# Sparse attention and a rational MLP on one core: new blocks for local and strided heads, transposes and loads moved between engines, and the last two chunks exchanged

## The chip, the cores and the metric

One of the eight cores of a Trainium2 chip runs the whole program. The metric is the device time of one execution in microseconds (us). Three executions of the kernel before took 433.36, 435.61 and 437.36 us; the median, 435.61 us, is the time before.

## The reference

Eight batches, eight heads, 576 positions, head size 64. Heads 0 to 3 are local (a query sees itself and the 31 keys ahead of it), heads 4 to 7 are strided (a query sees the earlier keys with the same position modulo 32). The result of attention, 4608 rows of 512, goes through two matrix products with a rational function between them:

```python
mask_local = (rel >= 0) & (rel < 32)
mask_strided = (rel >= 0) & (pos[None, :] % 32 == pos[:, None] % 32)
attn = softmax(where(mask, q @ k.T / 8, -1e9)); x = attn @ v     # (4608, 512)
h = x @ w_in                                                      # 512 -> 2048
g = (a0 + a1*h + a2*h**2 + a3*h**3) / (1 + |b0|*|h| + |b1|*h**2)
out = g @ w_out                                                   # 2048 -> 512
```

## The kernel before

Every instruction is recorded by `add(engine, ..., deps, cost, key)`. A list scheduler (`Program.schedule`) then fixes the order on each engine from those costs and keys; on the chip each engine works through its list in order and waits on semaphores. So a wait holds up all that stands behind it on the same engine. P = 36 is the step of the keys from one batch to the next.

**Attention of a batch.** `loads(b)` brings q, k and v from HBM on POOL's queue, with a cast to bf16: `qn`, `kn` (positions 0 to 511), `qm`, `km` (the last 64), `vt` and `v4` for local heads, `vs` and `w4` for strided ones; two buffers of each. `scores(b)` goes in rounds through a PSUM tile `psS` (batches 0 and 1 use `psA` and `psH` as well): TensorE transposes q and k with the identity `IDN` (`turn_s` for strided heads into `sT`, `turn_l` for local heads into `qL` and `kL`, `turn_m` for the last 64 positions), ScalarE or VectorE copies the result out. A score round then lays the mask into PSUM with two matmuls against `IDN`, adds the products of q and k, and ScalarE's Exp writes the probabilities. There are three strided rounds (`score_s`, into `ES`), two local ones (`score_l`, blocks of 128 queries by 128 keys, into `EL1`) and one for what crosses from block to block (`score_o`, into `EL2`, `EL3`). A position is split as p = 4*p' + g, with four residues g, so that a strided head needs only the keys of its own residue.

`attend(b)` makes five tiles T of 128 rows (T = 4 holds the last 64 positions): matmuls into `psA` (the 65th column of v is one and gives the sum), then VectorE's reciprocal (L747) and product (L749) into one of three buffers `XR`, then a DMA transpose on SP's queue (L764) into `XT`, which holds the features of one chunk in the partitions, two buffers. The tiles T = 4 of all batches are gathered in `XT8`. In a strided head a tile holds 32 rows of each residue, so `psA` gets them by 16 matmuls of 32 columns.

**The MLP.** Nine chunks of 512 rows; chunk 8 is `XT8`. `dense1(c)`: 16 groups of four matmuls through three PSUM banks `psH`, each copied to `HB` by ScalarE (L813); then VectorE makes the rational function in nine passes over up to eight groups (L821 to L852), with ScalarE's Ln and Exp (L833, L836) in place of the division. `dense2(c)`: four output tiles m of 16 matmuls into `psO`, copied to `OS` by ScalarE and stored by SP: four stores of 32 rows per tile (L867), for chunk 8 eight stores of 16 rows (L874). The last chunk uses four PSUM banks at once. `Win` and `Wout` come by one DMA each (L441, L445). TensorE starts with 14 matmuls on zeros, and in batch 0 one more stands behind each round.

Of the kernel before, what the change touches and what calls it, by code (L numbers as in the profile page):

```python
# [264 lines left out]
def bass_strided_sparse_attn__then__act_rational_pade_kernel(nc, q, k, v, moe_w_in, moe_w_out, moe_a, moe_b, out):  # L265
# [19 lines left out]
    EOFF = 5.0  # L285

# [6 lines left out]
    sT = A("sT", [128, 2, 2, 4, NP], BF)  # L293
    qL = A("qL", [128, 2, S], BF)
    kL = A("kL", [128, 2, S], BF)
    NV = 2
    vt = [A(f"vt{i}", [128, 4, 4, VS], BF) for i in range(NV)]
    v4 = [A(f"v4{i}", [64, 4, VS], BF) for i in range(NV)]
    w4 = [A(f"w4{i}", [128, 4, VS], BF) for i in range(NV)]
    vs = [A(f"vs{i}", [128, 4, 4, VS], BF) for i in range(NV)]  # L300
    NE = 2
    EL1 = [[A(f"EL1_{i}_{p}", [128, 2, 4, 128], BF) for p in range(2)] for i in range(NE)]
    EL2 = [A(f"EL2_{i}", [128, 2, 2, 4, 4, 32], BF) for i in range(NE)]
    EL3 = [A(f"EL3_{i}", [64, 2, 2, 4, 32], BF) for i in range(NE)]
    ESW = 8 * NP + 64
    ES = [A(f"ES_{i}", [128, 2, ESW], BF) for i in range(NE)]
# [4 lines left out]
    NXT = 2  # L311
    XT = [A(f"XT{i}", [128, NK1, CH], BF) for i in range(NXT)]
    XT8 = A("XT8", [128, NK1, B * 128], BF)
# [12 lines left out]
    ML1 = A("ML1", [128, 512], BF)  # L326
    ML2 = A("ML2", [128, 384], BF)
    MS1 = A("MS1", [128, 3 * NP], BF)
    MS2 = A("MS2", [128, 2 * NP + 64], BF)
# [11 lines left out]
    ar = np.arange(128)  # L341
    part = np.arange(128)
    d1 = (4 * (ar % 32) + ar // 32)[None, :] - part[:, None]
    m1 = np.where((d1 >= 0) & (d1 < STRIDE), 0.0, NEG)
    ml1 = np.tile(m1, (1, 4))
    ml2 = np.full((128, 2, 4, 4, 8), NEG)
    ml3 = np.full((128, 2, 4, 16), NEG)
    for g in range(4):
        for i in range(16):
            dd = 4 * i + g - part  # L350
            ok = (dd >= 0) & (dd < STRIDE) & (part < 64)
            ml3[ok, :, g, i] = 0.0
            dd = 128 + 4 * i + g - part
            ok = (dd >= 0) & (dd < STRIDE)
            if i < 8:
                ml2[ok, :, :, g, i] = 0.0
            else:
                assert not ok.any()
    ml2 = np.concatenate([ml3.reshape(128, -1), ml2.reshape(128, -1)], axis=1)
    dp = np.arange(NP)[None, :] - part[:, None]  # L360
    ms = np.where((dp >= 0) & (dp % 8 == 0), 0.0, NEG)
    ms1 = np.tile(ms, (1, 3))
    iq = np.arange(16)[None, :]
    ik = (part % 32)[:, None]
    mlo = np.where((ik < 16) & (iq >= ik) & ((iq - ik) % 8 == 0), 0.0, NEG)
    ms2 = np.concatenate([np.tile(ms, (1, 2)), np.tile(mlo, (1, 4))], axis=1)
# [17 lines left out]
    for dst, arr, nm, g_, ev in ((IDN, np.eye(128), "c_idn", gI, idn), (MS1, ms1, "c_ms1", gM, msk_ev),  # L384
                                 (MS2, ms2, "c_ms2", gM, msk_ev), (ML1, ml1, "c_ml1", gM, msk_ev),
                                 (ML2, ml2, "c_ml2", gM, msk_ev)):
# [29 lines left out]
    memset(ZB, OS[NO - 1][:, :], 0.0, key=-950.0)  # L416
    for i in range(NV):
        memset(vt[i], vt[i][:, :, :, 64:65], 1.0)
        memset(vs[i], vs[i][:, :, :, 64:65], 1.0)
        memset(v4[i], v4[i][:, :, 64:65], 1.0)  # L420
        memset(w4[i], w4[i][:, :, 64:65], 1.0)
    for i in range(NE):
        memset(EL2[i], EL2[i].rearrange("x a q t g c -> x (a q t g c)"), 0.0, cost=1.2)
        memset(EL3[i], EL3[i].rearrange("x a q g c -> x (a q g c)"), 1.0)

# [4 lines left out]
    ch_w1 = chan("c_w1")  # L430
    ch_w2 = chan("c_w2")
# [5 lines left out]
    g1 = ch_w1.group()  # L437
    g2 = ch_w2.group()

    def load_win():  # L440
        add("POOL", (lambda e: e.dma_start(Win[:, :, :], w_in.rearrange("(a p) f -> p a f", p=128))),  # L441
            [], 1.0, -960.0, g1, 12.0)

    def load_wout():
        add("POOL", (lambda e: e.dma_start(Wout[:, :, :], w_out.rearrange("(f p) o -> p f o", p=128))),  # L445
            [], 1.3, -900.0, g2, 12.0)

    def loads(b):
# [17 lines left out]
        if b == 0:  # L466
            for x, src, dst, dsm in srcs:
                big(x, src, dst, 4, 8, parts[x][0], key + x, 1.9)
            for x, src, dst, dsm in srcs:
                small(x, src, dsm, parts[x][1], key + 2 + x)  # L470
            for x, src, dst, dsm in srcs:
                big(x, src, dst, 0, 4, gg[x], key + 4 + x, 1.9)
            for x in range(2):
                n_ev[x, b] = {"s": parts[x][0].ops, "m": parts[x][1].ops, "l": gg[x].ops}
# [7 lines left out]
        base = [v_free[i], ini[id(vt[i])], ini[id(vs[i])], ini[id(v4[i])], ini[id(w4[i])]]  # L482
        key = (b - 1.9) * P if b > 1 else -990.0 + 50 * b
        for h in range(4):
            add("POOL", (lambda e, b=b, i=i, h=h: e.dma_start(  # L485
                vs[i][:, h, :, 0:64],
                v[b, 4 + h, 0:512, :].rearrange("(p g) d -> p g d", g=4))),
                base, 0.85, key, gv, 1.1)
        for g in range(4):
            add("POOL", (lambda e, b=b, i=i, g=g: e.dma_start(  # L490
                w4[i][32 * g:32 * g + 16, :, 0:64],
                v[b, 4:8, 512:576, :].rearrange("h (p g) d -> g p h d", g=4)[g])),
                base, 0.65, key, gv, 0.15)
        for h in range(4):
            add("POOL", (lambda e, b=b, i=i, h=h: e.dma_start(  # L495
                vt[i][:, :, h, 0:64],
                v[b, h, 0:512, :].rearrange("(t p) d -> p t d", p=128))),
                base, 0.85, key, gv, 1.1)
        add("POOL", (lambda e, b=b, i=i: e.dma_start(
            v4[i][:, :, 0:64],  # L500
            v[b, 0:4, 512:576, :].rearrange("h s d -> s h d"))),
            base, 0.7, key, gv, 0.5)
# [3 lines left out]
    s_free = [None]  # L506
    a_free = [None]
    h_free2 = [None]
    h_free = [None] * NHP
# [15 lines left out]
    q_free = [[]]  # L525
# [10 lines left out]

    def scores(b):
# [8 lines left out]
        ring = ["S", "A", "H"] if b == 0 else ["S", "A"] if b == 1 else ["S"]  # L546

# [6 lines left out]
        def turn_round(build, x, part, evacs):  # L554
# [6 lines left out]
            free[0] = [evac(eng, dst, src(ps), [o, q_free[0]], key, n) for eng, dst, src, n in evacs]  # L561
            return free[0]

        def score_round(msk, width, build, exps, deps):
# [5 lines left out]
            for (o, l, r) in build(ps):  # L570
# [4 lines left out]
            o2 = [add("ACT", (lambda c, dst=dst, src=src(ps): c.activation(dst, src, AF.Exp, scale=0.125)),  # L575
                      [o1, E_free[es]], 0.2 + n * 0.000833, key - EOFF) for dst, src, n in exps]
            free[0] = o2
            evs.extend(o2)


        dep = []
        depl = []

        def turn_s(x, eng):
            dep.append(turn_round(
                lambda ps: [mm(ps[:, gh, 128 * h:128 * h + 128], nat[x][:, 4 + h, 128 * gh:128 * gh + 128], IDN[:, :], True, True)
                            for gh in range(2) for h in range(4)],
                [x], "s", [(eng, sT[:, x, :, :, 0:128], lambda ps: ps.rearrange("x e (h p) -> x e h p", h=4), 1024)]))
# [13 lines left out]
        def turn_m():  # L602
            ev = turn_round(small, [0, 1], "m", [
                ("DVE", sT[:, :, :, :, 128:144].rearrange("x q e h p -> x q (e h) p"),
                 lambda ps: ps[:, :, 0:128].rearrange("x q (n p) -> x q n p", p=16), 256),
                ("DVE", qL[:, :, 512:576], lambda ps: ps[:, 0, 128:256].rearrange("x (a n) -> x a n", a=2), 128),
                ("DVE", kL[:, :, 512:576].rearrange("x a (p g) -> x a g p", g=4),
                 lambda ps: ps[:, 1, 128:256].rearrange("x (a g p) -> x a g p", a=2, g=4), 128)])
            dep.append(ev[0])
            depl.append([ev[1], ev[2]])  # L610

        def turn_l(x, eng):
            if x == 0:
                e = [(eng, qL[:, a, 0:512].rearrange("x (t g p) -> x g t p", t=4, g=4),
                      lambda ps, a=a: ps[:, a, :].rearrange("x (g t p) -> x g t p", g=4, t=4), 512) for a in range(2)]
            else:
                e = [(eng, kL[:, :, 0:512].rearrange("x a (p g) -> x a g p", g=4),
                      lambda ps: ps.rearrange("x a (g p) -> x a g p", g=4), 1024)]
            depl.append(turn_round(
                lambda ps: [mm(ps[64 * hh:64 * hh + 64, a, 128 * g:128 * g + 128],  # L620
                               nat[x][:, 2 * a + hh, 64 * g:64 * g + 64], IDN[:, :], True, True)
# [369 lines left out]
```

## Time and profile before

| what | value |
|---|---|
| median of three executions | 435.61 us |
| profiled execution, its own time | 437.65 us |
| its span, first to last instruction | 435.9 us |
| busy: TensorE, VectorE, ScalarE | 367.6, 329.0, 305.4 us |
| mean granted TensorE clock | 0.93 |
| first matmul of dense1, chunk 0 | 45.38 us |
| last copy of an output tile ends | 421.84 us |

Times inside an execution are counted from the start of the span. A busy share is taken over the whole span, and stages differ: at the start DMA works and the engines wait, in the middle three engines are almost full, at the end only stores are left. So the span is read stage by stage. In the views "x16" is a count of instructions, "a <- b" in front of a number names who was waited for, PEld is the load of weights, and SPq and POOLq are the queues that issue DMAs.

### The profile page before, as it was taken

What the parts mean: (1) busy time and instruction counts of PE and PEld (TensorE: products, weight loads), DVE (VectorE), ACT (ScalarE), POOL (GpSimd) and SP (SyncE); (2) the same over time, 40 slices, a digit from 0 to 9 for tenths busy, and PEclk for the clock granted to TensorE, in tenths of its full rate; (3) what the DMA queues carried; (4) which work ended last, traced back from release to release, by engine and by line L of the source; (5) the groups of instructions that cost most, each with busy time, mean ns of one, the idle gap of its engine ahead of it and who ended that gap; (6) DMA issues with size and microseconds to landing.
All of it is one profiled execution on the core that took longest, in us unless ns stands there. A gap on an engine that the chain in (4) does not pass through costs nothing.

```text
span 435.9 us, 7966 instructions
## 1 busy us (share of the span) xinstructions
PE 367.6 (84%) x3417; PEld 175.6 (40%) x3417; DVE 329.0 (75%) x309; ACT 305.4 (70%) x338; POOL 107.4 (25%) x144
## 2 busy tenths in 40 slices
PE   6751877679996999799989999999999997998760
PEld 2330332334552454355435444553454442343320
DVE  3421197960599589689996989796989999999920
ACT  2320398926794899789978897879897798849510
POOL 9985211008208402900580064000000000000000
PEclk9875698969999999999999999999999999899895
DMA  9999998029929923952594265221123101012012
GB/s 130 182 192 166 199 110 108 15 29 96 115 54 127 94 49 47 147 81 50 67 149 74 48 85 69 61 50 26 26 48 85 28 23 48 25 44 54 24 35 64
DMA packets 92260, 34.05 MB, mean 78 GB/s; under 512 B 66112, under 2 KB 87104, under 8 KB 92224
## 3 DMA queue, kind: packets, MB, share of 16 engines
q0 software_dynamic: 62144, 18.37, 42.0%
q1 hardware_dynamic: 30080, 15.16, 16.2%
q8 instruction: 27, 0.44, 0.5%
q14 instruction: 9, 0.07, 0.1%
HBM read 37.17 MB, written 9.44 MB: 107 GB/s over the span
## 4 chain that ended last, share of the span: by engine, by line
PE 49%; DVE 25%; DMA 11%; ACT 9%; issue 3%; SPq 1%; DVEq 0%
PE psH L518 20%; PE psO L518 14%; PE psS L518 10%; DMA XT<-XR 9%; PE psA L518 6%; DVE UU L827 4%; DVE T L852 3%; DVE T L843 3%; DVE T L847 3%; ACT kL L529 2%; DVE XR L749 2%; ACT UU L833 2%; DVE T L845 2%; DVE UU L824 2%; ACT UU L836 2%
## 5 line engine op out<-in xcount | busy, mean ns | idle before, releaser
L518 PE MATMUL psH<-XT,Win 128*128 128x512 bf16 x576 | 147.5, 393 | 18.9 <-DMA XT<-XR 16.8
L518 PE MATMUL psO<-Wout,T 128*128 128x512 bf16 x528 | 133.9, 384 | 8.7 <-ACT OS L917 4.9
L813 ACT ACTIVATE HB<-psH 128x512 bf16<-128x512 f32 x144 | 84.3, 600 | 58.8 <-PE psH L518 57.7
L518 PEld LDWEIGHTS psH<-XT,Win 128*128 128x128 bf16 x576 | 55.0, 100 | 87.0 <-issue 16.3
L833 ACT ACTIVATE UU<-UU,cst 128x2048 bf16<-128x2048 bf16 x36 | 71.5, 1998 | 7.1 <-DVE UU L827 7.0
L518 PEld LDWEIGHTS psO<-Wout,T 128*128 128x128 bf16 x528 | 47.1, 98 | 65.6 <-ACT OS L917 9.1
L836 ACT ACTIVATE UU<-UU 128x2048 bf16<-128x2048 bf16 x36 | 68.5, 1912 | 0.1
L821 DVE TENSOR_SCALAR T<-HB 128x4096 uint16<-128x4096 uint16 (+1 forms) x20 | 22.4, 1121 | 38.6 <-ACT HB L813 38.6
L852 DVE TENSOR_TENSOR T<-T,UU 128x4096 bf16<-128x4096 bf16 (+1 forms) x20 | 41.3, 2063 | 4.0 <-ACT UU L836 4.0
L485 POOL DMA_DIRECT2D vs<-in_v_dram x32 | 27.4, 861 | 63.9 <-PE psA L518 63.5
L847 DVE TENSOR_TENSOR T<-T,HB 128x4096 bf16<-128x4096 bf16 (+1 forms) x20 | 41.4, 2069 | 0.3
L827 DVE TENSOR_TENSOR UU<-UU,T 128x4096 bf16<-128x4096 bf16 (+1 forms) x20 | 41.4, 2069 | 0.3
L843 DVE TENSOR_TENSOR T<-T,HB 128x4096 bf16<-128x4096 bf16 (+1 forms) x20 | 41.3, 2067 | 0.2
L457 POOL DMA_DIRECT2D qn<-in_q_dram x9 | 8.7, 965 | 89.7 <-PE psS L518 88.9
L749 DVE TENSOR_TENSOR XR<-psA,RC 128x512 bf16<-128x512 f32 x40 | 27.4, 686 | 3.2 <-DMA XT<-XR 3.0
L917 ACT ACTIVATE OS<-psO 128x512 f32<-128x512 f32 x33 | 20.0, 606 | 12.7 <-PE psO L518 12.2
L495 POOL DMA_DIRECT2D vt<-in_v_dram x32 | 26.1, 847 | 0.0
L575 ACT ACTIVATE ES<-psS 128x864 bf16<-128x864 f32 (+1 forms) x20 | 17.0, 852 | 12.5 <-PE psS L518 11.0
L840 DVE TENSOR_SCALAR T<-HB,coef 128x4096 bf16<-128x4096 bf16 (+1 forms) x20 | 24.8, 1238 | 0.3
L824 DVE TENSOR_SCALAR UU<-T,coef 128x4096 bf16<-128x4096 bf16 (+1 forms) x20 | 24.6, 1230 | 0.3
L845 DVE TENSOR_SCALAR T<-T,coef 128x4096 bf16<-128x4096 bf16 (+1 forms) x20 | 23.6, 1182 | 0.3
L747 DVE RECIPROCAL RC<-psA 128x8 f32<-128x8 f32 x40 | 8.1, 203 | 20.8 <-PE psA L518 20.7
(111 smaller groups left out, 391.7 us busy)
## 6 DMA issues: line engine op xcount, KB each, us to landing
out_dram<-OS SPq DMA_DIRECT2D x128, 64.0 KB, 1.7
qn<-in_q_dram POOLq DMA_DIRECT2D x7, 512.0 KB, 6.8
kn<-in_k_dram POOLq DMA_DIRECT2D x7, 512.0 KB, 5.8
vs<-in_v_dram POOLq DMA_DIRECT2D x32, 64.0 KB, 6.3
vt<-in_v_dram POOLq DMA_DIRECT2D x32, 64.0 KB, 3.5
Win<-in_moe_w_in_dram POOLq DMA_DIRECT2D x1, 2048.0 KB, 13.4
Wout<-in_moe_w_out_dram POOLq DMA_DIRECT2D x1, 2048.0 KB, 26.2
out_dram<-OS SPq DMA_DIRECT2D x32, 32.0 KB, 1.7
```

Source lines behind the costliest of these rows:

```text
L485: add("POOL", (lambda e, b=b, i=i, h=h: e.dma_start(vs[i][:, h, :, 0:64], v[b, 4 + h, 0:512, :].rearrange("(p g) d -> p g d", g=4))), base ...
L518: return lambda e: e.matmul(out_ap, l, r, start=start, stop=stop, skip_group_check=True)
L749: o3 = add("DVE", (lambda d, rc=rc, x=x: d.tensor_tensor(x.rearrange("x (h d) -> x h d", h=8), psA[:, :, 0:64], rc[:, :, :].to_broadcast([ ...
L813: o2 = add("ACT", (lambda a, hb=hb, hi=hi, fi=fi: a.activation(hb[:, fi, :], psH[hi], AF.Copy)), [o1, hb_free[ig % NHB]], 0.6, key - HOFF)
L824: d2 = add("DVE", (lambda d, gn=gn, u=u, t3=t3: d.tensor_scalar(u[:, 0:gn, :], t3[:, 0:gn, :], b1_ap, b0_ap, op0=Alu.mult, op1=Alu.add)), ...
L827: d3 = add("DVE", (lambda d, gn=gn, u=u, t3=t3: d.tensor_tensor(u[:, 0:gn, :], u[:, 0:gn, :], t3[:, 0:gn, :], op=Alu.mult)), [d2], ctt, ke ...
L833: ln = add("ACT", (lambda a, u=u, sl=sl: a.activation(u[:, sl, :], u[:, sl, :], AF.Ln, bias=cst[:, 0:1], scale=1.0)), [d3, cons], 0.28 + H ...
L836: ex = add("ACT", (lambda a, u=u, sl=sl: a.activation(u[:, sl, :], u[:, sl, :], AF.Exp, scale=-1.0)), [ln], 0.28 + HG * CH * 0.000833, key ...
L843: d5 = add("DVE", (lambda d, gn=gn, hb=hb, t3=t3: d.tensor_tensor(t3[:, 0:gn, :], t3[:, 0:gn, :], hb[:, 0:gn, :], op=Alu.mult)), [d4], ctt ...
L845: d6 = add("DVE", (lambda d, gn=gn, t3=t3: d.tensor_scalar(t3[:, 0:gn, :], t3[:, 0:gn, :], a_ap[1], None, op0=Alu.add)), [d5], cts, key + ...
L847: d7 = add("DVE", (lambda d, gn=gn, hb=hb, t3=t3: d.tensor_tensor(t3[:, 0:gn, :], t3[:, 0:gn, :], hb[:, 0:gn, :], op=Alu.mult)), [d6], ctt ...
L852: d9 = add("DVE", (lambda d, gn=gn, t3=t3, u=u: d.tensor_tensor(t3[:, 0:gn, :], t3[:, 0:gn, :], u[:, 0:gn, :], op=Alu.mult)), [d8, lns], c ...
```

## The change

- **Local heads**: nine blocks of 64 queries by 96 keys (the 64 of the block and 32 ahead; `kL` gets zeros at both ends, `vt` becomes [96 keys, 9 blocks]). A block needs no second matmul for what crosses its edge, so `EL2`, `EL3`, `v4` and `score_o` go.
- **Strided heads**: a tile T < 4 now holds all 128 positions of residue T, so that four matmuls of 128 columns take the place of 16 of 32. Rows of local and strided heads stand in another order in `XT`; dense1 reads the two local parts of `XT` in runs of 16 elements. An output tile is then one residue, and one store of 128 rows takes the place of four.
- **Five mixed score rounds** in place of six: `score_0` (what is left of the last 64 strided positions, and six local blocks) into `E0`, and `score_1(h)` for h = 0 to 3 (strided head 4+h and three local blocks) into `E1`. Their order of work: `turn_l`, `turn_m`, `score_0`, then `score_1`.
- **Transposes**: from batch 2 on, `turn_s` becomes two DMA transposes of 128x1024 on SP's queue (`turn_sd`, L594). For batches 0 and 1 the transpose of `XR` goes from DMA to TensorE and ScalarE's copy. The tile T = 4 takes two smaller DMA transposes (`XT8l`, `XT8s`).
- **Buffers and parts**: three `XT` in place of two; `Win` in four DMAs, `Wout` in two, each with a semaphore of its own.
- **Order of chunks**: 0 to 6, then 8, then 7; in batch 7 tile T = 4 goes first.

```diff
+    TORD = {7: (4, 0, 1, 2, 3)}
+    XD = 2
+    XP = 2
...
-    NXT = 2
+    NXT = 3
...
+        def turn_sd(x):
+            g = ch_t[x].group()
+            o = add("SP", (lambda e: e.dma_start_transpose(
+                sT[:, x, :, :, 0:128].rearrange("x h g p -> x (h g) p"),
+                nat[x][:, 4:8, :].rearrange("x h c -> x (h c)"))),
+                [n_ev[x, b]["s"], st_old], 2.0, base - 20 + x, g, 1.2)
+            uses[x].append(o)
+            dep["s", x] = [o]
...
+        def local(ps, off, units):
+            return [(ps[:, hh, off + WIN * u:off + WIN * u + WIN],
+                     kL[64 * hh:64 * hh + 64, a, WIN * t:WIN * t + 128],
+                     qL[64 * hh:64 * hh + 64, a, WIN * t:WIN * t + WIN])
+                    for u, (t, a) in enumerate(units) for hh in range(2)]
...
+            if T < 4:
+                gh, j = divmod(T, 2)
+                for h in range(4):
+                    makers.append(mm(psA[:, 4 + h, 0:65], E1[es][:, h, j, gh * NP:gh * NP + 128],
+                                     vs[iv][:, h, T, 0:65], h == 0, True))
...
+            if b < XP:
+                bank, free = (psO, o_free) if (b or T % 2) else (psH[2], h_free3)
...
+                o4 = add("PE", makers, [o3, free[0]], 0.3, key - 1.0)
...
+    CORD = [0, 1, 2, 3, 4, 5, 6, 8, 7]
...
+                    elif kk < 2:
+                        r = XT[c % NXT][:, kk, :].rearrange("x (t g p) -> x g t p", g=4, p=16)
...
-            dst = out[576 * c + 128 * m:576 * c + 128 * m + 128, :].rearrange("(p g) o -> g p o", g=4)
-            for g in range(4):
-                add("SP", (lambda e, dst=dst, osl=osl, g=g: e.dma_start(
-                    dst[g], OS[osl][32 * g:32 * g + 32, :])), [ev], 0.75, key - 60, go, 0.2)
+            dst = out[576 * c:576 * c + 512, :].rearrange("(p g) o -> g p o", g=4)[m]
+            add("SP", (lambda e: e.dma_start(dst, OS[osl][:, :])), [ev], 0.75, key - 60, go, 0.9)
```

Two places show how the order moves. TensorE, from the fourth attention tile of batch 2 to the first dense1 matmuls of chunk 2, before (`vt0`, `vs0`: values of batch 2; `XT0` is chunk 2's, `XT1` chunk 1's, `T30` to `T32` hold chunk 0's function):

```order
L518 MATMUL psA<-vs0,ES_0 32x65 x16
L518 MATMUL psO<-Wout,T32 128x512 x4
L518 MATMUL psS<-IDN,qn1 64x128 x16
L518 MATMUL psA<-vt0,EL2_0 128x65 x4
L518 MATMUL psA<-v40,EL3_0 128x65 x4
L518 MATMUL psA<-vs0,ES_0 16x65 x16
L518 MATMUL psA<-w40,ES_0 16x65 x16
L518 MATMUL psO<-Wout,T30 128x512 x4
L518 MATMUL psS<-IDN,kn1 64x128 x16
L518 MATMUL psO<-Wout,T31 128x512 x4
L518 MATMUL psH<-XT0,Win 128x512 x4
```

Between the fourth tile and chunk 2 stand three groups of four dense matmuls, two turns and the fifth tile. The same place now (`XT2` is chunk 2's; the fourth tile and one group of chunk 1's dense1 stand just ahead of the first row):

```order
L511 MATMUL psO<-Wout,T32 128x512 x4
L511 MATMUL psS<-M1,IDN 128x480 x2
L511 MATMUL psS<-sT 128x144 x4
L511 MATMUL psS<-qL,kL 128x64 x6
L511 MATMUL psA<-vt0,E1_0 64x65 x4
L511 MATMUL psA<-vs0,E1_0 16x65 x16
L511 MATMUL psA<-w40,E0_0 16x65 x16
L511 MATMUL psS<-M1,IDN 128x480 x2
L511 MATMUL psS<-sT 128x144 x4
L511 MATMUL psS<-qL,kL 128x64 x6
L511 MATMUL psO<-Wout,T30 128x512 x4
L511 MATMUL psH<-XT2,Win 128x512 x4
```

Two whole score rounds of batch 3 have moved in between the fourth tile and chunk 2. On SP's queue, the transposes of batch 2's tiles and what stands among them, now (`sT<-qn0`, `sT<-kn0` are batch 4's):

```order
L768 DMA_TRANSPOSE XT2<-XR0 128x4x128
L768 DMA_TRANSPOSE XT2<-XR1 128x4x128
L875 DMA out_0_dram<-OS1 128x512
L594 DMA_TRANSPOSE sT<-qn0 128x8x128
L768 DMA_TRANSPOSE XT8l<-XR2 128x2x64
L768 DMA_TRANSPOSE XT8s<-XR2 128x2x128
L594 DMA_TRANSPOSE sT<-kn0 128x8x128
L875 DMA out_0_dram<-OS2 128x512
```

Before, this queue held only `XT` and `XT8` transposes and stores; now batch 4's transposes of q and k stand among them, and one of the stores and the fifth tile's transposes are behind a wait for batch 3's last score round.

More of the change, by code (lines that the diff above doesn't have):

```diff
@@ L338, in bass_strided_sparse_attn__then__act_rational_pade_kernel @@
     psO = Pa("psO", [128, 512], F32)
[L341 to L347, printed above, removed]
-    for g in range(4):
[L349 to L360, printed above, removed]
-    ms = np.where((dp >= 0) & (dp % 8 == 0), 0.0, NEG)
[L362 to L366, printed above, removed]
+    part = np.arange(128)[:, None]
+    wc = (4 * (np.arange(WIN) % 16) + np.arange(WIN) // 16)[None, :]
+    mw = np.where((wc - part + PADK >= 0) & (wc - part + PADK < STRIDE), 0.0, NEG)
+    dp = np.arange(NP)[None, :] - part
+    ms = np.where((dp >= 0) & (dp % 8 == 0), 0.0, NEG)
+    dp = np.arange(16)[None, :] - part
+    mlo = np.where((part < 16) & (dp >= 0) & (dp % 8 == 0), 0.0, NEG)
+    m0 = np.concatenate([np.tile(mlo, (1, 8)), np.tile(mw, (1, 6))], axis=1)
+    m1 = np.concatenate([np.tile(ms, (1, 2)), np.tile(mw, (1, 3))], axis=1)
     def const(name, arr):
@@ L612, in turn_l @@
+            dep["m"] = ev
         def turn_l(x, eng):
[L613 to L622 removed]
@@ L684, in scores @@
+        if by_dma:
+            turn_sd(0)
+            turn_sd(1)
+        turn_l(0, "ACT")
+        turn_l(1, "DVE" if b == 0 else "ACT")
         turn_m()
         if b == 0:
-            turn_l(0, "ACT")
-            turn_l(1, "DVE")
-        for r in range(3):
-            score_s(r)
+            score_0()
+        if not by_dma:
+            turn_s(0, "ACT")
+            turn_s(1, "DVE")
         if b:
-            turn_l(0, "ACT")
-            turn_l(1, "ACT")
-        for a in range(2):
-            score_l(a)
@@ L695, in scores @@
-        score_o()
+            score_0()
+        for h in range(4):
+            score_1(h)
         for x in range(2):
             n_free[x][i] = uses[x]
-        q_free[0] = list(evs)
+        st_free[0] = st_use
+        l_free[0] = l_use
         if b == 0:
@@ L791, in dense1 @@
         f0 = 0
-        for gn in sizes(c):
+        for gn in sizes(n):
             ig = ng[0]
```

366 lines of the change are left out of this document (182 added, 184 removed).

## The prediction

> **What bounds the kernel now.** I read the page first, then the busy time stage by stage, then who waited for whom, and last single stretches of the timeline.
>
> ```profile
> span 435.9 us, 7966 instructions
> PE   6751877679996999799989999999999997998760
> ...
> 45.00:100.00 55.00, 41.92 (x430) 19.60 (x433) 38.83 (x45) 36.49 (x39) 5.20 (x8) 0.82 0.74 91
> 100.00:320.00 220.00, 208.89 (x2203) 103.63 (x2202) 182.02 (x165) 185.49 (x212) 65.41 (x81) 0.99 0.61 75
> 320.00:416.00 96.00, 88.53 (x469) 38.48 (x467) 94.05 (x70) 73.39 (x75) 0.00 (x0) 0.96 0.16 41
> 416.00:435.90 19.90, 5.11 (x24) 2.14 (x22) 1.38 (x2) 1.19 (x2) 0.00 (x0) 0.76 0.22 53
> ```
>
> The columns of the last rows are the stretch, its length, then busy time of TensorE, its weight loads, VectorE, ScalarE and POOL, the granted clock, DMA. Four stages with four limits. Up to 45 us attention of batch 0 runs as one chain and nothing is full but DMA. From 100 to 320 us TensorE is the fullest, 208.9 of 220 us; VectorE (182.0) and ScalarE (185.5) each have over 34 us to spare. From 320 to 416 VectorE is full (94.05 of 96). After that only stores are left.
>
> **The start.**
>
> ```profile
> 14.14 0.83 POOL L441 DMA_DIRECT2D Win<-in_moe_w_in_dram  x1
> DMA to landing us min/median/max: 13.4/13.4/13.4
> 6.97 0.61 PE L518 MATMUL psS<-IDN,qn 128*128 128x128 bf16 x8
> 25.58 0.24 PE L518 MATMUL psA<-vt,EL_0_0 128*128 128x65 bf16 x2 [0.95 <-ACT EL_0 L575]
> 27.13 12.58 SPq L764 DMA_TRANSPOSE XT<-XR  x5
> 32.19 0.21 DVE L747 RECIPROCAL RC<-psA 128x8 f32<-128x8 f32 x1 [1.07 <-PE psA L518]
> 35.37 0.69 DVE L749 TENSOR_TENSOR XR<-psA,RC 128x512 bf16<-128x512 f32 x1 [2.98 <-DMA XT<-XR]
> 45.38 7.19 PE L518 MATMUL psH<-XT,Win 128*128 128x512 bf16 x20 [7.88 <-DMA XT<-XR]
> L813 ACT ACTIVATE HB<-psH 128x512 bf16<-128x512 f32 x144 | 84.3, 600 | 58.8 <-PE psH L518 57.7
> ```
>
> Attention's first tile starts at 25.58; the fourth has its sums at 32.40, but its product waits 3 us for a buffer that a DMA transpose still reads, and chunk 0 starts only at 45.38, behind DMA. `Win` is there at 14.1 + 13.4 = 27.5, so it isn't what chunk 0 waits for. With the change these transposes are on TensorE. The four tiles are spaced about 2.0 us now (the fourth's sums are 6.8 us behind the first tile's start); four transposes between them cost some 0.3 us (eight took 0.45, below), so the fourth sum comes at about 25.6 + 3 x 2.3 + 0.8 = 33.3 less what the rounds ahead gain. The rounds ahead run from 6.97 to 25.5 on three banks, 11 of them, 1.7 us each; now there are 10, so I take off 1.5: 31.8. Then 0.7 product, 0.35 transposes, 0.6 copy (the 600 ns row) and 0.2 of hops: **chunk 0 starts at 33.6, a gain of 11.8 us**. Bounds: 9 (no round saved, a late v, see below), 14 (two rounds saved and a faster pace). The parts of `Win` bring nothing here, since even the whole lands ahead of 33.6.
>
> **The middle, 100 to 320.** TensorE's share comes first, from starts in the timeline to the next start.
>
> ```profile
> 244.37 0.20 PE L518 MATMUL psA<-vt,EL_1_0 128*128 128x65 bf16 x1
> 244.71 0.30 PE L518 MATMUL psA<-vs,ES 128*32 128x65 bf16 x16
> 244.95 0.39 PE L518 MATMUL psO<-Wout,T 128*128 128x512 bf16 x1
> 253.08 0.29 PE L518 MATMUL psA<-vt,EL_1 128*128 128x65 bf16 x4
> 253.53 0.30 PE L518 MATMUL psA<-vs,ES 128*16 128x65 bf16 x16
> 253.98 0.39 PE L518 MATMUL psO<-Wout,T 128*128 128x512 bf16 x1
> 270.71 0.61 PE L518 MATMUL psS<-IDN,qn 128*128 128x128 bf16 x8
> 271.16 0.23 PE L518 MATMUL psA<-vt,EL_0_0 128*128 128x65 bf16 x2
> 271.61 0.39 PE L518 MATMUL psO<-Wout,T 128*128 128x512 bf16 x1
> ```
>
> Per batch from batch 2 on:
> - `turn_s` gone: 271.16 - 270.71 = 0.45, for q and k 0.90 us.
> - Tiles: T = 1 to 3 take 244.95 - 244.37 = 0.58 each (eight full matmuls 0.34, sixteen narrow ones 0.24), T = 0 takes 0.45, T = 4 0.90: together 3.09. Now T < 4 has 8 matmuls of 64 columns and 4 of 128. At 0.03 each (eight full ones in 0.34, less the 0.1 of the turn to the next kind) that is 0.46, and T = 4, with 4 and 32 narrow ones (0.45, from 253.53 to 253.98), 0.66: together 2.50. Gain 0.59; bounds 0 (if a 64-column one costs 0.055, as a 128-wide transpose does) and 1.1 (if two that fill different halves run side by side, as the narrow ones seem to).
> - Score rounds: masks are 4864 columns in place of 5248, at 0.42 ns a column (0.216 us per 512) and two products per unit as before: 0.16; one round less, which I estimate at twice the 0.1 us of a turn from one kind to the next: together 0.35, bounds 0 and 0.7.
>
> 1.84 us, for six batches 11.0. Then the waits:
>
> ```profile
> PE psH L518 <- DMA XT<-XR: 16.8, 4, 7.9
> 132.66 6.98 DMA XT<-XR
> 170.99 7.03 DMA XT<-XR
> 211.68 8.26 DMA XT<-XR
> L764 SPq DMA_TRANSPOSE XT<-XR x40: 1188/1190/2607, 27.1 to 335.2; - x40
> DMA to landing us min/median/max: 2.3/2.4/10.3
> ```
>
> Of 16.8 us that TensorE waited for `XT`, 7.88 is the start; 8.9 are three waits in the middle, ahead of chunks 2, 3 and 4 (in the chain of waits, the three rows with a start), where a transpose took 7 to 8 us to land in place of 2.4. With two rounds of scores moved in between (the order above) and a third `XT`, tiles stand further ahead of their chunk, and I count all three as gone. What is late next is the ScalarE copy that frees `psS` and `psH`, and VectorE: from 11.0 + 8.9 = 19.9 us at most I take two thirds, **13 us**. Bounds: 5 (VectorE and ScalarE hold TensorE back) and 20. That the other two can follow:
>
> ```profile
> L530 DVE CAST sT<-psS 128x1024 bf16<-128x1024 f32 x8 | 9.8, 1222 | 7.5 <-PE psS L518 7.4
> L530 DVE CAST qL<-psS 128x128 bf16<-128x128 f32 x7 | 2.0, 279 | 0.0
> L529 ACT ACTIVATE sT<-psS 128x1024 bf16<-128x1024 f32 x6 | 6.1, 1020 | 0.0
> 268.29 1.73 PE psH L518 x8
> 379.94 1.73 PE psH L518 x8
> ```
>
> each loses a copy of `sT` (1.22 and 1.02 us a batch, six batches), ScalarE two calls of Exp besides, and VectorE gains one small copy in `turn_m` (0.28 by the row of 128 columns). At two thirds, 100 to 320 shrinks to 207 us, for 182 - 6 x 0.94 = 176 us of VectorE: 85% busy, and it reached 98% in the stretch behind. Reading `XT` in runs of 16 costs nothing: chunk 5 (268.29) reads whole rows, chunk 8 (379.94) reads 16 of every 32, both eight matmuls in 1.73 us. The start of that stretch, 45 to 100, I move as a whole.
>
> The DMA transposes of `sT` are the one thing added to a queue. A 128x512 one holds SP 1.19 us, so 128x1024 should hold it 2.4 and land 3.6 after issue. A pair, with the two small `XT8` transposes between, is then about 8 us from batch 3's last score round to the landing; on TensorE 14 groups of four dense matmuls of 0.216 (1.73 for eight; 12 us), four tiles, two turns and `score_0` stand between that round and the first `score_1` of batch 4, about 17 us, and more for later batches. What queues behind on SP, `XT8` and a store, is needed late. So I cost it at nothing, by that cover; without it, 8 us a batch.
>
> The Trainium skill (“VectorE: DVE Perf Modes”, sections “The three transpose paths” and “Rules for kernel authors”) speaks against this move: 390 ns for a 128x128 block on TensorE, 1309 ns by DMA, and TensorE wherever PSUM will do as the destination. By that an `XT` transpose of four blocks would take an estimated 5.2 us if they went in turn; the trace has 2.4, so the trace doesn't bear it out here.
>
> **The end.**
>
> ```profile
> 419.18 14.93 SPq L874 DMA_DIRECT2D out_dram<-OS  x32
> 421.15 0.69 DVE L914 COPY OS<-psS 128x512 f32<-128x512 f32 x1 [1.03 <-PE psS L518]
> out_dram<-OS SPq DMA_DIRECT2D x32, 32.0 KB, 1.7
> DMA to landing us min/median/max: 1.6/1.7/6.4
> ```
>
> The last copy is done at 421.84, but SP needs 14.93 us for 32 stores of 16 rows, up to 434.1; the last lands 1.7 after its issue and the span ends at 435.9. Now the last chunk has four stores of 128 rows, one issue (0.45) per copy. Of 256 KB no row shows the landing: from 1.7 (32 KB) to 6.4 (the slowest store of all, the last row). I take 2.5, near the 1.7: 421.9 + 2.5 + 0.6 (what lay behind the last landing before) = 425.0. **Gain 10.9 us**, bounds 7 and 11.7. The 32 small stores now stand under the last chunk's work.
>
> **The sum.** 437.65 (own time of the profiled execution) - 11.8 - 13 - 10.9 = 401.95. That execution was 2.04 above the median of 435.61, so against the median: **400 us**.
>
> **The rivals.**
> 1. *The middle pays little*: TensorE's time is freed, but waits for ScalarE's copies and VectorE take its place, since all three are over 80% full. Only 5 us: 408. For it: 38 us of VectorE's idle time in the middle was there while TensorE was full. Against: 98% in the next stretch. Chance 0.16.
> 2. *The middle pays in full*, 20 us, and the start 12 or more: 392. Chance 0.10.
> 3. *The transposes of `sT` are late* (place: the first `score_1` of each batch from 2 on). Crowded, the five `XT` transposes of batch 0 took from 27.1 to 38.5 + 10.3 = 48.8 for 20 blocks of 128x128, 1.08 us each at most. The pair with `XT8` between is 20 blocks, 21.7 us against 17 of cover: 4.7 a batch, 28 in all, 428. From 1.15 us a block (23 us, 6 a batch) the whole gain is lost, and at 1.3 it is 26 us, 9 a batch, 54 in all: 454, slower. Against: the median of 40 landings is 2.4 us, also with POOL's loads under way. Chance 0.08, of which 0.03 for slower, 0.01 for no change; the rest lies between 412 and 430. The figure of the Trainium skill (“VectorE: DVE Perf Modes”, “The three transpose paths”), 1309 ns a block, lies on the slower side of that point.
> 4. *The start isn't shorter by that much*: `vt` now loads 768 rows a head in place of 512, and `Win` is in line behind it; if the first `Win` part comes at 38 in place of 27.5, chunk 0 starts there: 404 to 408. Chance 0.04.
>
> **How the numbers follow.** The forecast, 392 to 408, has 0.62; with rivals 1, 2 and 4 and their bounds 388 to 414, which leaves out rival 3 and little else, since not all bounds fall together (they would give 390 and 415). A measurement of this kernel can tell about 1% from no change. Only rival 3 gives that or slower: faster 0.95, same 0.02, slower 0.03.
>
> **What would show it.** Right: first dense1 matmul at 31 to 36; no wait of `psH` for `XT` over 2 us; TensorE's busy time down by 10 to 15 us; four stores at the end and the span's end 3 to 4 us behind the last copy; `score_1` waits for ScalarE, not for DMA `sT`. Wrong: rows "PE psS <- DMA sT" of several us each, or chunks 2 to 6 still 40 us apart.

## The result, and the profile after

| | before | after |
|---|---|---|
| median | 434.92 us (4 executions) | 398.15 us (396.04 to 398.39, 4 executions) |
| profiled execution, own time; span | 437.65; 435.86 us | 398.39; 396.59 us |
| first matmul of dense1, chunk 0 | 45.38 us | 34.95 us |
| last copy of an output tile ends | 421.84 us | 393.66 us |
| from there to the end of the span | 14.0 us | 2.93 us |

The ratio is 0.914 (95% interval 0.908 to 0.919). The spans differ by 39.3 us, in three parts: 10.4 at the start, 17.8 from the first dense1 to the last copy (called **the run of chunks** below), 11.1 behind the last copy. The page after, in the rows that stood for before:

```profile
span 396.6 us, 6915 instructions
PE 345.1 (87%) x2913; PEld 165.0 (42%) x2960; DVE 320.7 (81%) x309; ACT 300.5 (76%) x320; POOL 111.0 (28%) x148
PE   5667966379999999999998999999999799995796
```

Of 2960 matmuls this trace has 2913, so its TensorE time is a little low; an execution of the same kernel with all of them (run 9 below) has 351.5 us, against 367.6 before. TensorE's stages, by the busy time in stretches (columns as in the prediction), after:

```profile
100.00:320.00 220.00, 210.15 (x1892) 100.39 (x1924) 202.36 (x185) 190.82 (x200) 54.25 (x64) 1.00 0.71 91
```

The middle is still TensorE's, but VectorE went from 182 to 202 us of the same 220, and ScalarE from 185 to 191, since the same passes now fill a shorter time. For the run of chunks the same view gives, before and in the complete execution of the changed kernel (run 9):

```profile
45.38:421.84 376.46, 344.45 (x3112) 163.81 (x3112) 316.28 (x280) 296.57 (x327) 70.23 (x87) 0.96 0.50 68
```
```profile
33.45:391.73 358.28, 329.07 (x2698) 153.61 (x2690) 311.07 (x283) 289.90 (x308) 78.80 (x99) 0.95 0.67 85
```

18.2 us less, of which 15.4 is TensorE's busy time (344.45 to 329.07) and only 2.8 its idle time (32.0 to 29.2). The waits for a DMA after, and ahead of them the longest new wait of TensorE (who waited, for whom, us in total, times, longest):

```profile
PEld psO L511 <- DVE XR L737: 13.5, 6, 3.3
...
DVE coef L385 <- DMA coef<-in_moe_b_dram: 7.8, 1, 7.8
PEld psS L511 <- DMA qn<-in_q_dram: 2.0, 1, 2.0
PEld psA L511 <- DMA kn<-in_k_dram: 1.7, 1, 1.7
PE psS L511 <- DMA qn<-in_q_dram: 1.5, 1, 1.5
PE psA L511 <- DMA kn<-in_k_dram: 1.4, 1, 1.4
PEld psH L511 <- DMA XT<-XR: 0.6, 1, 0.6
```

The 16.8 us of `psH` for `XT` are down to one wait of 0.6, and no row says "DMA sT". The first row is what came in: the transposes of `XR`, which now stand on TensorE, wait there for VectorE's product, and hold up what is behind them. Its six waits lie at the start: two of 1.2 us in batch 0, ahead of the first dense1, and four of 2.3 to 3.3 in batch 1, at 70 to 84 us, ahead of chunk 1. The later batches have no such transposes. The tail of the timeline, after:

```profile
390.38 0.60 ACT L925 ACTIVATE OS<-psO 128x512 f32<-128x512 f32 x1 [5.38 <-PE psO L511]
391.00 3.02 SPq L875 DMA_DIRECT2D out_dram<-OS  x4
...
392.97 0.69 DVE L922 COPY OS<-psS 128x512 f32<-128x512 f32 x1 [1.03 <-PE psS L511]
```

Four stores, each behind its copy, and the span's end 2.93 us behind the last copy.

### The profile page after: what moved, and what is told of

Same layout as the page of the kernel before. It is cut to its first block, busy times and chain, and to the rows that moved or that the text cites. A ratio compares the mean times of both kernels' runs of the same rounds, so it can differ in the third digit from the quotient of the medians.

```text
span 396.6 us, 6915 instructions
## 1 busy us (share of the span) xinstructions
PE 345.1 (87%) x2913; PEld 165.0 (42%) x2960; DVE 320.7 (81%) x309; ACT 300.5 (76%) x320; POOL 111.0 (28%) x148
## 4 chain that ended last, share of the span: by engine, by line
PE 59%; DVE 23%; ACT 12%; DMA 3%; issue 2%; POOL 0%; POOLq 0%
PE psH L511 24%; PE psO L511 19%; PE psS L511 9%; PE psA L511 7%; DVE UU L836 4%; ACT kL L523 4%; DVE T L861 3%; DVE T L852 3%; ACT UU L842 3%; DVE T L856 3%; ACT HB L822 2%; DMA kn<-in_k_dram 2%; DVE T L830 2%; DVE UU L833 2%; DVE T L849 2%
## 5 line engine op out<-in xcount | busy, mean ns | idle before, releaser
L511 PE MATMUL psO<-Wout,T 128*128 128x512 bf16 x502 | 127.8, 379 | 11.4 <-ACT OS L925 6.2
L511 PE MATMUL psH<-XT,Win 128*128 128x512 bf16 x496 | 128.8, 390 | 2.6 <-ACT HB L822 1.2
L842 ACT ACTIVATE UU<-UU,cst 128x2048 bf16<-128x2048 bf16 x36 | 71.6, 1996 | 10.5 <-DVE UU L836 10.4
L511 PEld LDWEIGHTS psH<-XT,Win 128*128 128x128 bf16 x512 | 49.0, 100 | 60.5 <-issue 4.7
L476 POOL DMA_DIRECT2D vt<-in_v_dram x8 | 7.2, 900 | 75.9 <-PE psA L511 75.9
L925 ACT ACTIVATE OS<-psO 128x512 f32<-128x512 f32 x33 | 19.7, 598 | 10.3 <-PE psO L511 10.1
L480 POOL DMA_DIRECT2D vt<-in_v_dram x32 | 25.5, 815 | 0.0
L859 DVE TENSOR_SCALAR T<-T,coef 128x4096 bf16<-128x4096 bf16 (+1 forms) x20 | 24.1, 1206 | 0.1
L854 DVE TENSOR_SCALAR T<-T,coef 128x4096 bf16<-128x4096 bf16 (+1 forms) x20 | 23.4, 1171 | 0.2
```

What stands on the lines that cost most here:

```text
L511: return lambda e: e.matmul(out_ap, l, r, start=start, stop=stop, skip_group_check=True)
L842: ln = add("ACT", (lambda a, u=u, sl=sl: a.activation(u[:, sl, :], u[:, sl, :], AF.Ln, bias=cst[:, 0:1], scale=1.0)), [d3, cons], 0.28 + H ...
```

## The experiments

The kernel before took 436.45 us on the chip of runs 1 to 4, 432.57 on that of runs 5 to 8 and 436.16 on that of runs 9 to 12. Kernels are compared on one chip or by their ratio to before. On the chip of runs 5 to 8 the kernel before lay anywhere from 426.92 to 438.22, so the ratios there are good to 0.01 only, and the changed kernel itself was not run there. The first attention tile came at very different times in profiled executions of one kernel (22.06 us in run 2, 27.07 in run 10, both with `XP = 1`), so the start is read as the distance from that tile to the first dense1, and the chunks as the distance from there to the last copy.

**1 and 2: the `XR` transposes on TensorE.** Run 1 has `XP = 0` (none), run 2 `XP = 1` (batch 0 alone).

```diff
-    XP = 2
+    XP = 0     # run 2: 1
```

> The changed kernel, but the tiles of batches 0 and 1 go through DMA transposes again (XP = 0). My theory (chunk 0 waited for transposes landing in a crowded DMA): chunk 0's first dense1 matmul moves from 34.95 back to 43 to 47 us, and the whole gets 8 to 14 us longer, 406 to 412. Rival (the start is earlier for other reasons: fewer rounds, local heads first): under 3 us, about 400.

> The changed kernel with TensorE transposing the tiles of batch 0 only (XP = 1); batch 1 goes by DMA. From chunk 0 to chunk 1 the changed kernel took 4.9 us less than the one before, which the prediction counted as nothing. If that is due to batch 1's tiles no longer going by DMA: chunk 1 starts 3 to 6 us later, 401 to 404. If it is due to shorter score rounds and loads: within 1 us of 398.

Run 1: 401.80 us, ratio 0.923 (0.918 to 0.927). Run 2: 394.52 us, 0.905 (0.902 to 0.909). From first tile to first dense1: 17.1 us with DMA, 9.7 with TensorE, 9.7 in the changed kernel, 19.8 before. The waits of run 1 show the DMA on that path again:

```profile
PE psH L511 <- DMA XT<-XR: 6.5, 1, 6.5
DVE XR L737 <- DMA XT<-XR: 4.2, 2, 3.0
```

So batch 0's transposes are worth 7.4 us by the traces and 7.3 by the medians, a little less than the 8 at the low end of what was expected; run 1's time, 401.80, stayed below the 406 too, and against the changed kernel (0.923 for 0.914) only some 4 us are lost. Both answers expected of run 2 failed: without batch 1's transposes on TensorE nothing was lost, and its time lies below both.

**3: two `XT` buffers.**

```diff
-    NXT = 3
+    NXT = 2
```

> The changed kernel with two XT buffers in place of three. Theory of the prediction (third buffer and moved order together take away 8.9 us of waits of psH for XT): if the third buffer does it, waits of psH for DMA XT come back with 5 to 9 us, 403 to 407. If the moved order alone does it: under 1 us, 397 to 399.

396.21 us, 0.910 (0.904 to 0.916); waits for `XT` 0.3 us (TensorE) and 0.8 (its weight loads). The rival held: the third buffer brings nothing, and the order on every engine is the same without it as with it. What took the 8.9 us of waits away is the rest of the change, and the order that came with it.

**4: `sT` by TensorE in all batches.**

```diff
-    XD = 2
+    XD = 8
```

> The changed kernel with turn_s on TensorE for all batches (XD = 8, no DMA transposes of sT). Theory (TensorE is the fullest engine in the middle, 0.9 us a batch, and the two copies go to engines over 85% full): 4 to 8 us longer, 402 to 406. Rival (the DMA transposes cost as much on SP and in waits as they save): within 1 us or shorter, 395 to 399.

406.45 us, 0.933 (0.928 to 0.938): 10.2 us above run 3. The 16 transposes a batch on TensorE and their copies are back in six batches (TensorE is busy for 357.0 us, 5.5 more than in run 9, or 0.92 a batch where 0.90 was predicted), and a wait with them:

```profile
PE psH L511 <- DMA XT<-XR: 3.9, 1, 3.9
```

By its ratio it lies 8.4 us above the changed kernel, so moving these transposes to DMA is worth 8 to 10 us. Not all of it need be their own time: the order moves with them (chunk 2 starts 44.2 us behind chunk 1 in place of 36.7). In the changed kernel no row of waits names a DMA into `sT`, so all landed in their cover; the DMA issues (last column: median us from issue to landing) have

```profile
XT<-XR SPq DMA_TRANSPOSE x24, 2.5
sT<-qn SPq DMA_TRANSPOSE x6, 4.0
sT<-kn SPq DMA_TRANSPOSE x6, 3.7
```

and in run 9, the same kernel, 5.1 and 5.0 for the last two.

**5: the tiles' matmuls twice.** For T = 0 to 3 each matmul into `psA` is issued a second time (sums and products both double, their quotient stays).

```diff
...
+            if T < 4:
+                makers = makers + again     # the same 12 matmuls, accumulated
```

> The changed kernel, each matmul of the tiles T = 0 to 3 issued twice (sums and products double alike, so the output stays): 48 matmuls more a batch, some 0.36 us a tile, 1.45 us a batch, 11 us in all, on TensorE alone. Theory (TensorE is still the fullest engine in the middle, so what the tiles lost was worth its time): 6 to 11 us longer, 404 to 409. Rival (VectorE, 202 of 220 us busy after the change, holds the pace): under 3 us.

407.71 us, 0.947 (0.938 to 0.957); the run of chunks 367.0 us, 8.3 to 8.8 longer than in the changed kernel. Busy time between 100 and 320 us:

```profile
100.00:320.00 220.00, 213.04 (x2133) 105.78 (x2166) 190.97 (x178) 180.25 (x189) 54.88 (x64) 0.99 0.69 87
```

TensorE stays full at 213.0 of 220 (213.1 in run 9) and the two others fall from 202 and 191 to 191.0 and 180.3: they wait for TensorE, and work added to it comes out in the time. It is no exact price: the scheduler sees the added cost, so the order moves too, and from the first tile to the first dense1 12.0 us passed in place of 9.7.

**6, 7 and 8: the end.** Run 6 is the changed kernel with the chunks in their old order, run 7 the kernel before with chunk 8 ahead of 7, run 8 the changed kernel with four stores of 32 rows per tile.

```diff
-    CORD = [0, 1, 2, 3, 4, 5, 6, 8, 7]
+    CORD = [0, 1, 2, 3, 4, 5, 6, 7, 8]      # run 6, and TORD = {}; run 7 the other way in the kernel before
...
-            add("SP", (lambda e: e.dma_start(dst, OS[osl][:, :])), ...
+            for g in range(4):                                               # run 8
+                add("SP", (lambda e, g=g: e.dma_start(
+                    dst[32 * g:32 * g + 32, :], OS[osl][32 * g:32 * g + 32, :])), ...
```

> The changed kernel with the chunks in order 0 to 8 (and tile T = 4 last in batch 7): the last chunk is stored by 32 DMAs of 16 rows again. Theory (SP's issues are the end): the span's end is 14 us behind the last copy in place of 2.9, 408 to 411. Rival (the exchange moves other work as well and the stores are a part only): 400 to 405.

> The kernel before with the exchange of chunks 7 and 8 alone: the last chunk is stored by 16 DMAs of 32 rows, four behind the last copy. Theory: the end behind the last copy shrinks from 14.0 to about 4 us, 425 to 427 where the kernel before has 436. Rival (chunk 7 last makes the last chunk wait for something): no gain, 434 to 437.

> The changed kernel with each output tile of chunks 0 to 7 stored by four DMAs of 32 rows in place of one of 128. Theory (only what stands behind the last copy counts): 1 to 2 us longer, 399 to 400. Rival (SP's queue is in the way of the transposes in the middle, now that those of sT stand in it): 3 us or more, over 401.

Run 6: 404.99 us, 0.944 (0.932 to 0.955). Run 7: 427.79 us, 0.991 (0.985 to 0.996), 4 to 5 us below before. Run 8: 399.12 us, 0.928 (0.918 to 0.938). The stores of the last chunk (start, and how long SP issues them), in the timelines of runs 6, 7 and 8:

```profile
386.22 14.68 SPq L881 DMA_DIRECT2D out_dram<-OS  x32
```
```profile
415.97 7.79 SPq L870 DMA_DIRECT2D out_dram<-OS  x16
```
```profile
387.67 7.70 SPq L876 DMA_DIRECT2D out_dram<-OS  x16
```

The end comes 13.8 us behind the last copy with 32 stores, 7.0 and 6.8 with 16, 2.93 with four. A store of 32 or 64 KB takes SP 0.46 to 0.49 us, and the copies of the last chunk come 0.86 us apart, so four stores per copy pile up and one doesn't. Hence the 11 us split: 7 from the exchange of the chunks, 4 from the tile that is one residue. I had expected the exchange alone to leave 4 us, and run 8 to lose 1 to 2; both are wrong, by the queue of 16. Run 6's time lies in its rival's range (400 to 405) and run 8's in its theory's (399 to 400), but on a chip where the kernel before took 4 us less; by the traces, run 6's end lies as far behind the last copy as its theory said, and run 8 loses 3.9 us there, not 1 to 2. In run 7 the time fell by 4 to 5 us where the end shrank by 7; where the rest went was not found. In run 8 the chunks kept their distances (38.9, 35.4, 38.2, 37.4, 41.2 us from the first `HB` of one to that of the next, from chunk 2 on, as in the changed kernel): SP is nowhere else in the way.

**9 to 12: batch 1 once more, the keys' copy, whole weights.** Run 9 is the changed kernel, run 10 has `XP = 1`. Run 11 has `XP = 1` too and lets the transposes of k write PSUM in the order in which `kL` holds them. Run 12 loads each weight by one DMA.

```diff
-                dst = kL[:, :, PADK:PADK + 512].rearrange("x a (p g) -> x a g p", g=4)        # run 11
-                to = lambda ps, hh, a, g: ps[64 * hh:64 * hh + 64, a, 128 * g:128 * g + 128]
+                dst = kL[:, :, PADK:PADK + 512]
+                to = lambda ps, hh, a, g: ps[64 * hh:64 * hh + 64, a, :].rearrange("x (p g) -> x g p", g=4)[:, g]
...
-    NG1, NG2 = 4, 2
+    NG1, NG2 = 1, 1                                                                           # run 12
```

> The changed kernel itself once more, as the measure for the three beside it. 396 to 400 us; first dense1 matmul 31.7 to 35, since the start of the attention lay anywhere from 22.0 to 25.3 us in the executions so far and the first dense1 follows it by 9.7; from there to the last copy 356.5 to 359; 2.9 us from the last copy to the end.

> XP = 1: only batch 0 of chunk 0 by TensorE, batch 1 by DMA. Theory: it is really faster, because batch 1's transposes no longer take a place on TensorE and psO's buffers between the first dense1 and chunk 1: 2 to 5 us below the changed kernel in this call, with the same distance of 9.7 us from the first attention tile to the first dense1, and some 52 us between the first HB of chunk 0 and that of chunk 1. Rival: the earlier run's 3.6 us were its earlier start (the first attention tile at 22.06 for 25.27); then both are within 1 us here as soon as their starts agree.

> As the one before, and turn_l's keys are written to PSUM in the order of residues, so that the copy to kL is contiguous on both sides (it took 2456 ns on ScalarE, the same copy for queries 1020). Theory: ScalarE gets 1.4 us a batch back, 22 of 300 us; TensorE bounds the chunks, so 0 to 2 us less than XP = 1 alone. Rival 1: ScalarE is what the scores wait for in many rounds, then 3 to 8 us. Rival 2: transposes that write PSUM in steps take longer on TensorE (four 128-column writes for 64 rounds), then 1 to 4 us more.

> The changed kernel with each of the two weights in one DMA instead of four and two. The prediction gave the parts nothing. Theory: within 1 us of the changed kernel, since the weights have long landed when the first dense1 starts at 31.7 to 35. Rival: the whole Win lands later than its first quarter and chunk 0 waits for it: first dense1 or the first HB 1 to 4 us later, with a DMA wait on Win's row.

| run (6 executions each) | median, lowest to highest | ratio to before | first tile to dense1; run of chunks |
|---|---|---|---|
| 9, changed kernel | 397.89 (396.15 to 400.58) | 0.916 (0.911 to 0.921) | 9.7; 358.3 us |
| 10, `XP = 1` | 395.93 (393.70 to 398.29) | 0.910 (0.906 to 0.915) | 9.7; 356.8 us |
| 11, `XP = 1`, keys' copy | 389.25 (388.28 to 390.98) | 0.896 (0.892 to 0.900) | 9.4; 353.5 us |
| 12, whole weights | 389.49 (388.23 to 390.53) | 0.896 (0.892 to 0.900) | 9.7; 350.5 us |

*Run 10* stays unsettled: 2.0 us less in the medians, but the intervals overlap, and at the same mean granted clock (0.948) one execution of each lies at 394.3 and 394.1. Batch 1 is not dearer by DMA; that it is cheaper was not shown.

*Run 11* fell to the first rival. The copy shrinks as meant, the transposes grow. Groups by line, of run 10 and of run 11:

```profile
L523 ACT ACTIVATE kL<-psS 128x1024 bf16<-128x1024 f32 x6 | 14.7, 2454 | 5.2 <-PE psS L511 5.2
L511 PE MATMUL psS<-IDN,kn 128*64 128x128 bf16 x96 | 4.2, 237 | 0.0
```
```profile
L511 PE MATMUL psS<-IDN,kn 128*64 128x128 bf16 x96 | 7.2, 342 | 0.0
L523 ACT ACTIVATE kL<-psS 128x1024 bf16<-128x1024 f32 x6 | 6.1, 1022 | 7.3 <-PE psS L511 7.3
```

The order on every engine is the same in both runs. TensorE pays 3.0 us of busy time for these transposes, and still the run of chunks is 3.3 us shorter, because it no longer waits for this copy: its idle time there falls from 29.1 to 24.4 us. Run 10's waits for it, of which run 11 has none left on `psS` and 1.5 us on `psA`:

```profile
PEld psS L511 <- ACT kL L523: 6.2, 5, 1.3
PEld psA L511 <- ACT kL L523: 3.3, 1, 3.3
```

The chain of waits had said so on both pages of the changed kernel: run 10's reads, and run 11's has lost the row "ACT kL L523 4%":

```profile
PE psH L511 25%; PE psO L511 20%; PE psS L511 10%; PE psA L511 7%; DVE T L852 4%; ACT kL L523 4%; DVE T L861 4%; DVE T L856 3%; DVE UU L836 3%; DVE T L849 2%; DMA kn<-in_k_dram 2%; DVE T L854 2%; DVE UU L833 2%; DVE T L830 2%; ACT HB L822 1%
```

4% of 396.5 us is 16 us, nearly all of ScalarE's seven copies of 2.45. Not all of the 6.7 us between the medians is the copy's, since the granted clocks differ: 0.934 to 0.956 in run 10's executions, 0.952 to 0.956 in run 11's. At 0.956 the spans are 391.9 us in run 10 and 386.5 to 387.7 in run 11, 4.2 to 5.4 less. The traces of run 2 (the same kernel as run 10) and of run 11 both have 1.00 over the first 25 us, and agree: the first dense1 at 31.75 and 30.73, the run of chunks 357.5 and 353.5. Ahead of the first dense1 one such copy stands, batch 0's on VectorE (2433 ns, now 1224).

*Run 12* fell out of both columns: 8.4 us faster. `Win` whole lands 13.2 us after its issue in place of 9.0 a part, and no row waits for it, so the parts do bring nothing, as predicted. But the list scheduler books each weight DMA on its one planned ring, 3.2 us for each of four parts and 6.3 for each of two; the edit left these figures as they were, so that the plan now has the loads of batch 1 land 9.6 us earlier and those of batch 2 another 6.3, and the order on TensorE is another. So this run changes two things, and it is the order that shows: behind the first dense1 no wait of TensorE in run 9 is for a load of q, k, v or weights, so an earlier landing alone had nothing to shorten there. Busy time from the first dense1 to chunk 1, to the last chunk in line, to the last copy, in runs 9 and 12:

```profile
33.45:84.60 51.15, 35.95 (x380) 19.02 (x372) 39.73 (x48) 38.82 (x40) 15.34 (x22) 0.73 1.13 128
84.60:337.30 252.70, 245.10 (x2117) 114.39 (x2118) 222.89 (x198) 215.68 (x232) 63.46 (x78) 0.99 0.69 86
337.30:391.73 54.43, 48.02 (x205) 20.20 (x203) 48.45 (x38) 35.41 (x36) 0.00 (x0) 0.94 0.13 40
```
```profile
35.36:86.30 50.94, 41.09 (x438) 20.43 (x434) 40.15 (x48) 41.59 (x45) 18.10 (x26) 0.73 1.30 146
86.30:333.60 247.30, 237.98 (x2030) 111.43 (x2029) 223.26 (x197) 210.71 (x227) 60.80 (x73) 1.00 0.64 82
333.60:385.83 52.23, 46.98 (x212) 20.02 (x212) 48.89 (x39) 35.29 (x37) 0.00 (x0) 1.00 0.15 46
```

The first stretch is as long in both, but run 12 does 5.1 us more on TensorE in it (438 matmuls for 380): attention that run 9 does later (the keys' copies of batches 1 to 3 start at 39.7, 65.6 and 90.2 us for 47.8, 78.1 and 104.0), in the full stretch, which is now 7.1 us less busy and 5.4 us shorter. (The 2.2 us of the last stretch come with a granted clock of 1.00 in place of 0.94.) One place of the timeline, runs 9 and 12:

```profile
37.13 5.34 PE L511 MATMUL psH<-XT,Win 128*128 128x512 bf16 x24
42.41 0.64 PE L511 MATMUL psS<-IDN,qn 128*64 128x128 bf16 x16
...
50.33 1.04 PE L511 MATMUL psA<-IDN,qn 128*128 128x128 bf16 x8 [3.23 <-ACT kL L523]
```
```profile
32.69 1.06 PE L511 MATMUL psS<-IDN,qn 128*64 128x128 bf16 x16
...
42.24 0.62 PE L511 MATMUL psA<-IDN,qn 128*128 128x128 bf16 x8 [0.52 <-ACT kL L523]
42.70 0.61 PE L511 MATMUL psS<-IDN,kn 128*128 128x128 bf16 x8
43.14 1.03 PE L511 MATMUL psH<-XT,Win 128*128 128x512 bf16 x4
```

In run 9 chunk 0's dense1 runs in a block and batch 1's scores behind it, with 3.23 us of waiting for the keys' copy; in run 12 the turns come ahead, and score rounds stand between groups of four. That the booked landing is what turned the order is read from the scheduler's code; a run with the parts and the smaller figures, or whole weights with the larger, was not made. Runs 11 and 12 both beat the two kernels (0.896 of before); the two edits together were not run.

## Why the prediction held, point by point

It said 400 us, 388 to 414; 398.15 came. Its three terms summed to 35.7 us, the spans differ by 39.3. The medians differ by 36.8 only, since the profiled execution before lay 2.7 us above its median and the one after 0.2; so part of the 400's closeness is luck.

- **The start**, 11.8 predicted, 10.4 measured (bounds 9 to 14). Its working needs 33.6 less 24.1, 9.5 us, from the first tile to the first dense1, and 9.7 came; run 1 shows that this is the transposes' doing, 17.1 without. The "1.5" for one round less does not appear in the two profiles (first tile at 25.27 for 25.58), but the granted clock over the first 25 us was 0.86 after and 0.93 before. At 0.93, in runs 3 and 9 (the same order), the first tile came at 23.5 and 23.8, 1.8 to 2.1 earlier than before, and run 9's first dense1 at 33.45, 11.9 earlier. So the miss of 1.4 goes with the clock, and the working held.
- **The middle**, 13 predicted, 17.8 measured for the whole run of chunks (bounds 5 to 20). By place, from the first dense1 to the first `HB` of chunk 1, to that of the seventh chunk, to the last copy, before and in run 9:

```profile
45.38:103.60 58.22, 45.51 (x467) 21.36 (x468) 39.21 (x45) 38.20 (x42) 8.39 (x12) 0.84 0.75 90
103.60:301.00 197.40, 186.29 (x2007) 92.77 (x2006) 163.92 (x151) 167.07 (x189) 61.84 (x76) 0.99 0.64 78
301.00:421.84 120.84, 112.64 (x640) 49.69 (x638) 113.15 (x85) 91.30 (x97) 0.00 (x0) 0.97 0.16 40
```
```profile
33.45:84.60 51.15, 35.95 (x380) 19.02 (x372) 39.73 (x48) 38.82 (x40) 15.34 (x22) 0.73 1.13 128
84.60:271.90 187.30, 182.97 (x1793) 87.08 (x1794) 158.88 (x153) 161.70 (x174) 63.46 (x78) 0.99 0.87 100
271.90:391.73 119.83, 110.15 (x528) 47.51 (x526) 112.46 (x83) 89.38 (x95) 0.00 (x0) 0.97 0.14 43
```

  The second row is the middle that was meant, and it lost 10.1 us (10.9 in the first profile after), near the 13. Its waits went as said: TensorE's idle time fell from 11.1 to 4.3 us, the 8.9 for `XT` are down to 0.2, and what is left is ScalarE's copy that frees `psS` (3.7 us for the keys'), which "what is late next" had named. Its busy time fell by 3.3 alone, less than two thirds of 11.0, because work came in from the ramp: before, 28 matmuls of dense2 and nine score rounds stood ahead of chunk 1, in run 9 none and five. Over the run of chunks busy time fell by 15.4, more than the 11.0. So the size of the term was right, and its split between busy time and waits was not. **The step that failed is "the start of that stretch, 45 to 100, I move as a whole"**: the ramp became 4.8 us shorter (7.1 in run 9). That work is gone from it, but its idle time rose from 12.7 to 15.2 us, 7.3 of it in waits for `XR`. Run 12 shows that another order fills some of it, and with it the run of chunks is 7.8 us shorter than in run 9.
- **The tiles** were predicted to fall from 0.58 to 0.46 us each on TensorE. The timeline after has 156.69 - 156.31 = 0.38, below that; T = 4 took 0.69 to 0.76 in run 9 (0.66 predicted). That makes some 0.9 us a batch, between the 0.59 taken and the bound of 1.1:

```profile
156.31 0.32 PE L511 MATMUL psA<-vt,E_0 96*64 96x65 bf16 x8
156.56 0.29 PE L511 MATMUL psA<-vs,E_0 128*128 128x65 bf16 x4
156.69 0.81 PE L511 MATMUL psH<-XT,Win 128*128 128x512 bf16 x3
```

- **The third `XT`** was named beside the new order as what removes the waits. Run 3: it does nothing.
- **The `sT` transposes at no cost, by their cover.** They landed in 3.7 to 4.0 us (5.0 to 5.1 in run 9; 3.6 said), nothing waited for them, and run 4 prices the move at 8 to 10 us gained. The rule of the Trainium skill weighed there (“VectorE: DVE Perf Modes”, “Rules for kernel authors”: TensorE, where PSUM will do) didn't decide here: TensorE was the full engine, so a DMA with cover was cheaper.
- **The end**, 10.9 predicted, 11.1 measured. 256 KB landed in 2.4 us (2.5 said). Runs 6 to 8 give the parts that the prediction hadn't split: 7 and 4.
- **The rivals.** Rival 1 (ScalarE and VectorE hold TensorE back) is partly true, run 11 found one of its places; run 5 shows that TensorE is still the bound. Rival 2 did not come: the start gave under 12 and the middle under 20. Nor did rivals 3 and 4: no "DMA sT" row, no wait for `Win`.

## What to carry to other kernels

When an engine is full in one stage and waits in the one before, look first for work of the full stage that can run earlier: run 12 gained 8 us with another order of the same work. Where a static scheduler books the landings of loads, these figures enter its order, so compare them with the landings in the trace. Read each copy in the chain of waits by its share, even on an engine with time to spare: "ACT kL 4%" was a 2.4 us copy behind which TensorE stood. At the end of a program, count the stores behind the last copies against the queue's time per store.

## What the hardware showed that I had not expected

- The same copy from PSUM takes ScalarE 1022 ns when it writes runs of bf16 and 2454 ns when it writes every fourth element; VectorE 1224 and 2433. The other way round, transposes that write every fourth f32 of PSUM show 342 ns for 237 in the group's mean (medians behind 100 us: 314 for 219). The Trainium skill (“SBUF — State Buffer”, “Specifications (TRN2)”; “PSUM — Partial Sum Buffer”, the same section) has 16-byte lines in SBUF that want two hits, and 8-byte ones in PSUM, where access patterns that are not contiguous slow matmuls; the direction agrees for PSUM, while for the copy (two bf16 per 16 bytes) that rule would see no loss, and the measurement has a factor of 2.4.
- One kernel doesn't start alike each time, and the start goes with TensorE's granted clock over the first 25 us. With the same work up to there the first attention tile came at 22.06 us at 1.00 (run 2), 23.76 at 0.93 (run 9), 25.27 at 0.86 (after) and 27.07 at 0.73 (run 10). So two traces' starts are compared at one clock, or not at all. The whole span follows the mean clock in the same way: 397.5 to 398.8 us at 0.931 to 0.936 and 394.3 at 0.948 in run 9. What sets the clock there was not found.
